# The last fold in pieces with a gate ahead of its transposes, finer weight turns and one more yield in a Fourier-mixing and expert kernel

## Chip, cores, metric

The kernel runs on one core of a Trainium2 chip. The metric is the time of the device in microseconds (us) for one execution; less is better. Each kernel was executed several times on one chip together with the kernel before, so that the two can be compared on the same chip. Each run has a state, fast or slow; on this one core a run counts as slow when it is over 1.5% above the fastest of its kernel. Medians and ranges below are of all runs of a kernel, ratios of its fast runs alone.

The engines are called as the profile calls them: PE is the tensor engine's matmuls (PEld its weight loads), DVE the vector engine, ACT the scalar engine, POOL GpSimd, SP the engine that issues most of the strip transfers. PSUM buffers are the buffers into which PE writes its results; to evict one is to copy it out, so that it can be used again. The granted clock is the share of full speed at which PE was allowed to run; where it is half, the text calls PE or the stretch cold, and warm where it is full.

## The reference

Two layers follow each other. The first takes the real part of a two-dimensional Fourier transform of each of 8 batches (2496 x 256). The second gives each of the 19968 rows to one of 8 experts, greedily by score and with equal capacity, and puts the row through that expert's two matrices. The code is shortened:

```python
def _attn_ref(x):                       # x: 8 x 2496 x 256
    X = np.fft.fft(x, axis=1)
    X = np.fft.fft(X, axis=2)
    return X.real.astype(np.float32)

def _moe_ref(x, w_gate, w1, w2):        # x: 19968 x 256, w1: 8 x 256 x 1024
    cap = N // E
    order = np.argsort(-(x @ w_gate).flatten())
    for idx in order:                   # greedy, each row once, each expert at most cap rows
        tok, e = (int(idx) // E, int(idx) % E)
        if assigned[tok] >= 0 or counts[e] >= cap:
            continue
        assigned[tok] = e
        counts[e] += 1
    # ... (cut: stop when all are assigned)
    for e in range(E):
        mask = assigned == e
        out[mask] = np.maximum(x[mask] @ w1[e], 0.0) @ w2[e]
```

## The kernel before

The program runs in stages, and these names are used throughout:

1. *Batches.* For each batch, DVE folds the rows with their mirror images (tiles `xa`, `xb`), PE transposes the result (`tp`) and multiplies it with the gate (`yps`), ACT copies.
2. *Logits.* PE transforms the gated columns along the sequence (`lps_...`).
3. *Selection and transform.* DVE chooses the rows of each expert by search, ranks and masks. Meanwhile PE computes the transform of the rows in 40 half-steps that are called units (`fftps`), and DVE, ACT and POOL combine them into strips which go to DRAM. PE also turns the first weights of four experts (`wps`: each turn is eight matmuls in four pairs, and each pair is evicted by ACT).
4. *Experts.* PE gathers, sorts (`sps`) and multiplies (`hps`, `ops`). In its midst an inverse list is built from one-hot matrices (`inv_ps`).

The last batch, as the kernel before emits it:

```python
for b in range(B):
    a_t, b_t = ab.pop(b)
    nc.vector.tensor_tensor(a_t[:, :, :, 1:D], a_t[:, :, :, 1:D], b_t[:, :, ::-1, D - 1:0:-1], op=AL.add)
    nc.vector.tensor_tensor(a_t[:, :, :, 0], a_t[:, :, :, 0], b_t[:, :, ::-1, 0], op=AL.add)
    # ... (cut)
    if b == B - 1:
        # ... (cut: the memory of xb is given to the weights)
        load_w1(0)
        load_w1(1)
        load_w2(wts[0])
        load_w2(wts[0])
    # ... (cut: copies and combinations of ACT and DVE)
    zts[b] = [turn_x(b, pv, 0), turn_x(b, pv, 1)]      # transposes of chunks 0 and 1
    if b > 0:
        gate_x(b - 1, zts.pop(b - 1))                  # gate of the batch ahead
    zts[b].append(turn_x(b, pv, 2))                    # transposes of chunk 2
    # ... (cut)
```

While the selection runs, the order of PE's work is decided when the program is built, by two counters of estimated time, `clock["PE"]` and `clock["D"]` (DVE). A `yield` with a number is so much DVE work; `yield SYNC` marks the place of a PE instruction of the selection, which waits for DVE.

```python
def unit():
    cost = next(units, None)
    if cost is not None:
        clock["PE"] += 1.15
        clock["D"] += cost
        clock["n"] += 1
        if clock["n"] in (18, 22, 28, 34):
            turn_w((18, 22, 28, 34).index(clock["n"]), "A")   # a whole expert in one block
            clock["PE"] += 2.0
    return cost is not None

for c in first_chain():
    if c is not SYNC:
        clock["D"] += c
        while clock["PE"] < clock["D"] - 1.0 and unit():
            pass
        continue
    # ... (cut: the same filling, then both counters are set to the later one)
```

In the expert stage, each yield of the generator `inverse` lets PE go on with one more part of other work before the inverse's own matmuls:

```python
yield 0.9
yield SYNC
for c in range(8):
    nc.tensor.matmul(inv_ps[:, 0:w], lhsT=o_lo[:, :, c], rhs=o_hi[:, c, :], ...)
```

## Time and profile before

| | kernel before |
|---|---|
| plain runs, median of 3 | 548.45 us (547.43 to 548.97) |
| profiled run, span | 591.5 us |
| PE busy | 482.5 us, 82% of the span |
| first expert matmul | at 173.79 us |
| longest wait of PE in the expert stage up to 360 us | 5.40 us, at the inverse |

The head of the profile's page: the busy time of each engine with its share of the span, and two rows of the span in 40 slices of 14.8 us. A digit is the busy share of a slice in tenths; PEclk is the granted clock of PE in tenths, so 9 is full.

```profile
PE 482.5 (82%) x4014; PEld 358.1 (61%) x4023; DVE 383.4 (65%) x1063; ACT 341.7 (58%) x786; POOL 310.8 (53%) x362
...
PE   0567778887899999998998798887787679687993
...
PEclk9998779999999999999999799999998989989997
```

The selection and transform lie in slices 7 to 11, where PE has sevens to nines, mostly eights; the expert stage behind them is nearly full up to the middle. From about 360 us on (slice 25) there are sevens and eights again, which the plain runs can hardly have had: the profiled execution was 43 us longer than they were. Behind 345 us PE has 17 waits of over 1 us in this profile, 30.8 us in sum. In the hole that is shown here PE, DVE and ACT are all idle for 1.7 us, and the profile does not name what ended it. The table of stretches shows it (window, its length, then the busy us of PE, PEld, DVE, ACT and POOL with counts, granted clock, share and GB/s of the DMA engines):

```profile
448.00:450.00 2.00, 0.37 (x3) 0.10 (x1) 0.00 (x0) 0.00 (x0) 0.52 (x1) 1.00 0.26 94
```

Why some executions have these holes, and on two chips all that were profiled, is not settled here. They are in kernels with and without the change. So what the change does is read from the first 340 us, in which the profiles are alike, and from times on one chip.

### The profile page before, as it was taken

The numbers are of one execution on the slowest core, as the hardware profiler recorded it, in microseconds if no ns is written. First come the engines' busy times: TensorE is split into PE (matmuls) and PEld (weight loads), VectorE is DVE, ScalarE is ACT, GpSimd is POOL, SyncE is SP. The second block draws the span as 40 slices with busy tenths as digits, with TensorE's granted clock in tenths as the row PEclk, the third lists the DMA queues.
The fourth block names the chain that finished last, engine by engine and source line by source line (L and its number), as shares of the span: only waits on it lengthen the run. The fifth ranks groups of instructions, "written<-read, shape, count | busy, mean of one in ns | idle before, by whom it ended". The sixth has DMA issues, their size and how long they took to land. (4 is left out here: it accounts for less than half of the span.)

```text
span 591.5 us, 11322 instructions
## 1 busy us (share of the span) xinstructions
PE 482.5 (82%) x4014; PEld 358.1 (61%) x4023; DVE 383.4 (65%) x1063; ACT 341.7 (58%) x786; POOL 310.8 (53%) x362
## 2 busy tenths in 40 slices
PE   0567778887899999998998798887787679687993
PEld 0444447775686667766765676655565457465772
DVE  7799864978889889798888762543332324343551
ACT  7789861454688778786777476443432334343551
POOL 7878540622226545343444245665666575656553
PEclk9998779999999999999999799999998989989997
DMA  8999835387698962222222223212222221112111
GB/s 270 314 282 305 252 62 83 109 292 207 203 280 162 240 148 90 91 94 89 89 90 95 69 89 98 71 54 76 66 65 70 67 75 55 61 53 66 65 55 48
DMA packets 35169, 74.63 MB, mean 126 GB/s; under 512 B 6115, under 2 KB 14349, under 8 KB 35104
## 3 DMA queue, kind: packets, MB, share of 16 engines
q0 software_dynamic: 23296, 42.10, 27.4%
q1 hardware_dynamic: 11808, 31.73, 15.9%
q8 instruction: 33, 0.54, 0.4%
q14 instruction: 32, 0.26, 0.1%
HBM read 51.26 MB, written 32.24 MB: 141 GB/s over the span
## 5 line engine op out<-in xcount | busy, mean ns | idle before, releaser
L990 ACT ACTIVATE hb<-hps 128x384 bf16<-128x384 f32 (+1 forms) x331 | 145.8, 492 | 77.1 <-PE hps L1229 61.0
L1252 PE MATMUL ops<-w2t,hb 128*128 128x256 bf16 (+1 forms) x1344 | 178.1, 277 | 0.1
L1252 PEld LDWEIGHTS <-hb 128*128 128x128 bf16 (+1 forms) x1344 | 134.3, 100 | 35.2 <-issue 1.9
L1256 POOL DMA_INDIRECT out_dram<-zball,rid x94 | 96.2, 1024 | 109.6 <-ACT zball L990 96.2
L1229 PE MATMUL hps<-xs,zball 128*128 128x384 bf16 x640 | 131.5, 330 | 19.3 <-issue 10.5
L1229 PEld LDWEIGHTS <-zball 128*128 128x128 bf16 x896 | 86.6, 99 | 87.0 <-issue 48.2
L994 DVE TENSOR_SCALAR hb<-hps 128x384 bf16<-128x384 f32 (+1 forms) x117 | 62.4, 546 | 69.4 <-PE hps L1229 45.2
L1229 PE MATMUL hps<-xt,zball 128*128 128x384 bf16 (+1 forms) x256 | 51.4, 329 | 16.8 <-issue 10.9
L990 ACT ACTIVATE zball<-ops 128x256 f32<-128x256 f32 x96 | 36.9, 385 | 46.8 <-PE ops L1252 26.0
L129 POOL DMA_INDIRECT xb<-in_x_dram,mir_i x40 | 53.0, 1326 | 14.0 <-issue 10.8
L285 PE MATMUL tp<-identf,xa 128*128 128x128 f32 x160 | 28.6, 345 | 21.2 <-issue 11.6
L990 ACT ACTIVATE xs<-sps 128x384 bf16<-128x384 f32 x73 | 32.4, 493 | 20.0 <-PE sps L1093 11.5
L285 PEld LDWEIGHTS tp<-identf,xa 128*128 128x128 f32 x160 | 24.2, 180 | 28.8 <-issue 13.9
L1093 PE MATMUL sps<-pt,xl 128*128 128x192 bf16 x320 | 34.4, 248 | 2.8 <-DVE pt L1071 1.8
L1021 POOL COPY stage<-stage 128x258 bf16<-128x258 bf16 x40 | 17.7, 446 | 35.8 <-DVE stage L1016 32.6
L1071 DVE TENSOR_SCALAR pt<-rampw,spot 128x193 bf16<-128x193 bf16 x160 | 32.2, 293 | 1.0 <-PE sps L1093 0.7
L1093 PEld LDWEIGHTS <-xl 128*128 128x128 bf16 x320 | 27.5, 99 | 8.1 <-issue 6.0
L1256 POOL DMA_INDIRECT out_dram<-zball,rows_l x23 | 22.3, 971 | 17.0 <-DVE zball L996 9.9
L996 DVE COPY zball<-ops 128x256 f32<-128x256 f32 (+1 forms) x21 | 8.9, 423 | 30.0 <-PE ops L1252 9.6
L1205 POOL DMA_INDIRECT xg<-t_dram,ids_l x24 | 23.1, 964 | 7.9 <-issue 7.9
L1019 ACT ACTIVATE stage<-stage 128x254 bf16<-128x254 bf16 x40 | 15.7, 414 | 15.8 <-DVE stage L1016 13.9
L287 ACT COPY zt<-tp 128x1024 f32<-128x1024 f32 (+1 forms) x24 | 20.2, 868 | 6.1 <-PE tp L285 6.1
(357 smaller groups left out, 783.5 us busy)
## 6 DMA issues: line engine op xcount, KB each, us to landing
t_dram<-stage SPq DMA_DIRECT2D x20, 512.0 KB
xl<-t_dram SPq DMA_DIRECT2D x20, 512.0 KB
xa<-in_x_dram SPq DMA_DIRECT2D x8, 1024.0 KB
w1raw<-in_moe_w_dram POOLq DMA_DIRECT2D x8, 512.0 KB
w2t<-in_moe_w_dram POOLq DMA_DIRECT2D x8, 512.0 KB
xa<-in_x_dram SPq DMA_DIRECT2D x8, 224.0 KB
out_dram<-zball,rid POOLq DMA_INDIRECT x94
xb<-in_x_dram,mir_i POOLq DMA_INDIRECT x40
```

The source lines that it names most:

```text
L129: nc.gpsimd.indirect_dma_start(out=bv[0:n, i, :], out_offset=None, in_=x_pairs, in_offset=bass.IndirectOffsetOnAxis(ap=mir_i[0:n, b * NK + ...
L285: nc.tensor.transpose(tp[:, blk, u, :], pv[:, 4 * c + u, blk * P:(blk + 1) * P], identf)
L287: nc.scalar.copy(zt[:, :, 0:nn, :], tp[:, :, 0:nn, :])
L990: nc.scalar.activation(dst, src, ACT.Relu if relu else ACT.Copy)
L994: nc.vector.tensor_scalar(dst, in0=src, scalar1=0.0, scalar2=None, op0=AL.max)
L1021: nc.gpsimd.tensor_copy(st[:, :, 1 + q, 0:P + 1], st[:, :, 3 * q, 0:P + 1])
L1071: nc.vector.tensor_scalar(marks[n][:, f, 0:EW + 1], in0=rampw[:, 0:EW + 1], scalar1=spot[:, c:c + 1], scalar2=None, op0=AL.is_equal)
L1093: nc.tensor.matmul(sps[:, j2 * EW:(j2 + 1) * EW], lhsT=xl[:, 2 * g + cc, j2 * P:(j2 + 1) * P], rhs=pt[:, 2 * g + cc, 0:EW], start=(cc == 0 ...
L1205: nc.gpsimd.indirect_dma_start(out=xg[0:nr, q, :], out_offset=None, in_=t_dram, in_offset=bass.IndirectOffsetOnAxis(ap=d["ids"](q, nr), ax ...
L1229: nc.tensor.matmul(hps[:, 0:n], lhsT=w1t[d["e"]][:, j2, fc * P:(fc + 1) * P], rhs=d["x"](j2), start=(j2 == 0), stop=(j2 == 1))
L1252: nc.tensor.matmul(ops[0:nr, 0:D], lhsT=d["hid"][:, fc, b0:b0 + nr], rhs=w2t[d["e"]][:, fc, :], start=(fc == 0), stop=(fc == F // P - 1))
L1256: put = nc.gpsimd.indirect_dma_start(out=out, out_offset=bass.IndirectOffsetOnAxis(ap=d["rows"](b0 // P)[0:nr], axis=0), in_=ot[0:nr, :], ...
```

## The change

Its intent was to shorten three places where PE waits: 2.29 us under the last fold, 1.51 and 2.10 us in the weight turns and 5.40 us at the inverse, in the profile before. The last fold goes in three pieces, so that the first transposes need not await all of it, and the gate of the batch ahead goes in front of those transposes, with its matmuls in another order (both halves of a chunk after each other). The weight turns of the first four experts go in sixteen pieces of two matmuls, one behind each of sixteen chosen units, so that no block of eight fills the PSUM buffers or stands in front of the search. And the inverse gets one more yield before its first matmuls.

```diff
     def gate_x(b, zts):
-        for blk in range(2):
-            for c, zt in enumerate(zts):
+        for c, zt in enumerate(zts):
+            for blk in range(2):
...
     for b in range(B):
         a_t, b_t = ab.pop(b)
-        nc.vector.tensor_tensor(a_t[:, :, :, 1:D], a_t[:, :, :, 1:D], b_t[:, :, ::-1, D - 1:0:-1], op=AL.add)
-        nc.vector.tensor_tensor(a_t[:, :, :, 0], a_t[:, :, :, 0], b_t[:, :, ::-1, 0], op=AL.add)
+        for i0, i1 in ((0, 2), (2, 4), (4, NK)) if b == B - 1 else ((0, NK),):
+            nc.vector.tensor_tensor(a_t[:, i0:i1, :, 1:D], a_t[:, i0:i1, :, 1:D], b_t[:, i0:i1, ::-1, D - 1:0:-1],
+                                    op=AL.add)
+            nc.vector.tensor_tensor(a_t[:, i0:i1, :, 0], a_t[:, i0:i1, :, 0], b_t[:, i0:i1, ::-1, 0], op=AL.add)
...
+        if b == B - 1:
+            gate_x(b - 1, zts.pop(b - 1))
         zts[b] = [turn_x(b, pv, 0), turn_x(b, pv, 1)]
-        if b > 0:
+        if 0 < b < B - 1:
             gate_x(b - 1, zts.pop(b - 1))
...
             yield SYNC
+            if c0 == 0:
+                yield SYNC
             for c in range(8):
                 nc.tensor.matmul(inv_ps[:, 0:w], ...)
...
     (turn_pieces is the body of turn_w, with a yield behind each pair of matmuls)
+    TURNS = (*range(15, 23), *range(26, 30), *range(33, 37))
+    pieces = (None for e in range(4) for _ in turn_pieces(e, "A"))
...
-            if clock["n"] in (18, 22, 28, 34):
-                turn_w((18, 22, 28, 34).index(clock["n"]), "A")
-                clock["PE"] += 2.0
+            if clock["n"] in TURNS:
+                next(pieces)
+                clock["PE"] += 0.45
```

More of the change, by code (lines that the diff above doesn't have):

```diff
@@ L1047, in turn_w, with turn_pieces @@
     def turn_w(e, eng=None):
+        for _ in turn_pieces(e, eng):
+            pass
+    def turn_pieces(e, eng=None):
         for j in range(2):
@@ L1055, in turn_w @@
                 take(w1t[e][:, j, fs], wps, eng=eng)
-        if e + 2 < E:
-            load_w1(e + 2)
+                if j == 1 and fh == 1 and e + 2 < E:
+                    load_w1(e + 2)
+                yield
     flat = [zball[:, b].rearrange("p i d -> p (i d)") for b in range(B)]
```

## The prediction

> **What bounds the kernel now.** I read four views: the stretches table (busy time of each engine in chosen windows), to see which engine is full where; the timeline around the last fold; the timeline around the weight turns; and the waits of the tensor engine (PE). The profiled execution took 591.5 us and the plain runs 548.45 us, so profiled stretches are up to 8% long in sum; I use differences only. Three rows of the stretches table (window, its length, then busy us of PE, PE weight loads, DVE, ACT, POOL, with counts):
>
> ```profile
> 62.00:82.00 20.00, 12.80 (x73) 8.05 (x74) 17.56 (x24) 15.95 (x36) 6.39 (x5) 0.77 0.44 141
> 125.00:152.00 27.00, 20.13 (x148) 14.16 (x149) 22.41 (x60) 13.07 (x28) 6.41 (x14) 1.00 0.61 180
> 174.00:200.00 26.00, 25.88 (x184) 17.44 (x185) 24.23 (x86) 21.94 (x54) 14.14 (x16) 1.00 1.02 205
> ```
>
> Up to about 150 us the PE has holes (12.80 of 20, 20.13 of 27); from there on it is full (25.88 of 26), and the chain that ended last is PE matmuls back to 355 us. So a microsecond in which the PE does not stand idle before the expert tiles, or between them, is a microsecond off the end; a microsecond won on DVE alone is not.
>
> The last batch (timeline):
>
> ```profile
> 78.86 2.81 DVE L343 TENSOR_TENSOR xa<-xa,xb 128x2550 f32<-128x2550 f32 x1
> 81.86 3.65 PE L285 MATMUL tp<-identf,xa 128*128 128x128 f32 x16 [2.29 <-issue]
> 85.44 2.33 PE L295 MATMUL yps<-zt,g_sb 128*32 128x512 f32 x12
> 88.83 1.91 PE L295 MATMUL yps<-zt,g_sb 128*32 128x512 f32 x12
> 92.67 0.19 PE L452 MATMUL lps_cE<-yhl,hi_cE 128*128 128x64 bf16 x1 [0.74 <-DVE yhl L309]
> ```
>
> The fold starts as soon as DVE is free (the DVE timeline shows no idle before it), so no load bounds it. PE idles 2.29 us under it, then transposes, does the gate of batch 6, then batch 7's gate, and the logits begin at 92.67. All is one chain.
>
> The weight turns and the late wait (timelines, and two more rows):
>
> ```profile
> 126.41 1.46 PE L1053 MATMUL wps<-w1raw,mt_b 128*128 128x512 bf16 x5
> 129.38 0.59 PE L1053 MATMUL wps<-w1raw,mt_b 128*128 128x512 bf16 x2 [1.51 <-ACT zball L990]
> 130.04 0.22 DVE L660 SCALAR_TENSOR_TENSOR s_low<-misc,s_part,s_lo 128x1 f32<-128x1 f32 x1 [1.65 <-PE misc L658]
> 136.72 0.22 DVE L660 SCALAR_TENSOR_TENSOR s_low<-misc,s_part,s_low 128x1 f32<-128x1 f32 x1 [1.95 <-PE misc L658]
> 151.69 0.59 PE L1053 MATMUL wps<-w1raw,mt_b 128*128 128x512 bf16 x2 [2.10 <-ACT zball L990]
> 328.46 0.64 PE L761 MATMUL inv_ps<-o_eq,oh 128*128 128x48 bf16 x8 [5.40 <-DVE o_eq L757]
> ```
>
> A turn's eight matmuls come in one block. The block outruns its three PSUM buffers and waits for ACT (1.51 and 2.10 us), and the search's one-column matmul (misc) behind it keeps DVE waiting (1.65, 1.95 us). At 328.46 the PE has waited 5.40 us, its longest wait of the expert stage, for the first one-hot of the inverse list.
>
> [...] 16 transposes take 1.94 us at 72.55 but 3.65 us at 81.86, and the granted clock of 62 to 82 us is 0.77. [...] In two narrow windows of batch 7's gate:
>
> ```profile
> 89.70 0.62 PE L295 MATMUL yps<-zt,g_sb 128*32 128x256 f32 x3
> 89.71 1.03 PE L295 MATMUL yps<-zt,g_sb 128*32 128x512 f32 x4
> ```
>
> A 256-wide matmul of chunk 2, the last in program order, starts at 89.70, while two 512-wide ones written before it still start after 90.1 (the group ends at 90.74). [...] I expect the new order to keep the 1.91 us. [...]
>
> **The change, part by part.**
>
> *Fold in pieces.* [...] Neighbours overlap by some 85 ns (78.86 to 81.76 is 2.90 for 2.985), five times instead of once: about 3.2 us, ending near 82.06 instead of 81.76. DVE loses 0.3 us, but pieces for chunks 0 and 1 are ready near 80.2 and 81.5. That readers wait for a slice only is visible elsewhere: the ACT copy of the stage tile starts at 109.52, before DVE's second write of that tile ends at 110.08.
>
> *Gate 6 first.* Its last input (the ACT copy at 79.03 to 79.61) is there, so it fills the PE's idle: 79.65 to 81.56 if warm, to about 83.1 if cold. Then, warm: transposes 81.5 to 83.45 (16 x 121 ns); ACT does the border copy after the fold (82.05), the two gate copies (to 82.95), the chunk copies of 1.0 us to 83.9 and 84.85; the last four transposes follow the first copy, then the place step to 85.05; batch 7's gate runs 84.95 to 86.85. From the gate's end to the logits took 90.74 to 92.67 = 1.93: logits near 88.8, a gain of 3.9. If the clock drops near 79.5, as it did before: gate 6 ends at 83.1, and the logits come near 90.2, a gain of 2.5. I take 3.3.
>
> *Weight turns.* I replayed the program's own pacing counters, which decide where units go. Before, 30 units (1.11 us of PE each) and three turns are issued in the first selection; after, 29 units and twelve pieces (the same three turns). Two pieces (2 x 0.43 us) now stand before the first search, which starts 0.87 later; the two search answers come near 129.2 and 132.7 instead of 130.04 and 136.72, and DVE reaches the strip marks about 4.7 us earlier. But PE is what counts. Idle removed: 1.51 + 2.10 in the turns, 0.53 at the rank matmuls, 0.28 at a stage buffer. Idle added: DVE's threshold and mask steps are no longer covered (1.30 to about 1.6, 0.99 to 2.0), about 0.8 behind one late piece eviction, 0.4 at a rank buffer, and 1.1 when a unit needs a PSUM buffer whose combine is queued behind the strip marks. That is 4.4 removed against 3.6 added, 0.8. Followed step by step to equal work (30 units, three turns), PE arrives near 153.3 instead of 154.4: 1.1. The fourth turn saves perhaps 0.4, which ACT, then nearly full, may take back. I take 1.1 in all.
>
> *One more yield in the inverse.* PE gets one more part of work ahead of the first inverse matmuls: eight sorting matmuls (0.66), six up (0.97), eight down (0.87) = 2.5 us off the 5.40. The remaining 3 us still cools the clock, as the 5.4 did, so I add nothing for it. The late gathers start one part later and are far from needed.
>
> Sum: 3.3 + 1.1 + 2.5 = 6.9 us. The rest of the program stays in order and PE-bound. 548.45 - 6.9 = 541.5.
>
> **Rivals.** (a) The gate's column groups serialize in the new order[...]. Then each gate has four steps of 0.43 per large chunk, about 3.5 us instead of 1.9; with gates 6 and 7 both on the chain the first part gains 0.7 at most, the total 4.3: 544. The narrow windows speak against it. (b) The units trade one wait for another: DVE's gain becomes PE idle at its masks and PSUM buffers, and twelve short evictions fill ACT. Then the turns give nothing or cost 1: 542.5 to 543.5. For it speaks that PE's idle sum hardly changes in my replay. (c) The saved DVE time does come through, because PE waits on DVE later (the waits of the expert stage up to 360 us, the inverse aside, sum to only 6.6 us): a turn gain near 4 makes 538.5. (d) The clock: PE stays warm through the last batch and the shorter inverse wait saves the half-rate stretch (sorting 1.45 against 0.82, up 2.08 against 1.14, 1.6 us): 539.5.
>
> **Range and chances.** The three gains are 2 to 4, -0.5 to 3 and 1.5 to 4; not all at one end. That makes 538.5 to 545. Faster by over 2% means under 537.5, a gain of 11, for which all three must be at their best: 0.08. A loss over 2% needs a mechanism that I see nowhere: 0.01.
>
> **What would show it.** In the profile after: no PE idle of 2 us before the last transposes, gate 6 ahead of them, and the first logits matmul 2.5 to 3.9 us earlier; one gate still near 1.9 us when warm (near 3.5: rival a). No wait of PE in the turns on ACT over 1 us, search answers without a DVE wait on misc near 1.7, and new PE waits on the masks near 2 us. The inverse wait near 3 us instead of 5.4. The prediction is wrong if the logits come less than 1.5 us earlier, if the PE reaches the first expert tile no earlier relative to the logits than before (rival b) or over 3 us earlier (rival c), or if the inverse wait stays.

## The result, and the profile after

The changed kernel is correct. It takes 543.83 us (median of 4 runs, 543.31 to 545.83), against 548.55 us of the kernel before beside it. Ratios here are the mean time of one kernel's fast runs over that of the other's in the same rounds, so they are not quite the ratio of the medians. The ratio is 0.9924, with a 95% interval of 0.9895 to 0.9953: 4.7 us faster, which is "the same" by the measure that counts only changes over 2%. It lies inside the predicted range, 2.3 us slower than the predicted 541.5.

The head of the page after, span 542.1 us, slices of 13.6 us:

```profile
PE 469.0 (87%) x4023; PEld 355.7 (66%) x4023; DVE 387.2 (71%) x1067; ACT 345.2 (64%) x786; POOL 312.4 (58%) x362
...
PE   0667777796899999999899989999999999999970
...
PEclk9997889999999999999999998999999999999995
```

The late slices are at nine or above: this execution has no late holes. Comparing the two spans would credit the change with 49 us; the comparison has to be made mark by mark.

The last batch in the timeline after (start us, duration us, engine, source line, operation, output<-inputs, sizes, count, and in brackets the idle time before it and what ended it):

```profile
77.78 1.21 DVE L344 TENSOR_TENSOR xa<-xa,xb 128x1020 f32<-128x1020 f32 x1
...
79.10 1.92 PE L295 MATMUL yps<-zt,g_sb 128*32 128x512 f32 x12
...
80.95 1.97 PE L285 MATMUL tp<-identf,xa 128*128 128x128 f32 x16
...
84.16 1.92 PE L295 MATMUL yps<-zt,g_sb 128*32 128x512 f32 x12
...
88.03 0.19 PE L456 MATMUL lps_cE<-yhl,hi_cE 128*128 128x64 bf16 x1 [0.74 <-DVE yhl L309]
```

The gate of batch 6 now stands before the transposes and takes 1.92 us, as does that of batch 7 in the new order. The transposes run at full clock (1.97 us instead of 3.65). From the fold's first piece to the logits it is 88.03 - 77.78 = 10.25 us, where it was 92.67 - 78.86 = 13.81.

Behind that, three waits of PE decided the rest. They lie inside the logits, at the threshold of the selection, and at the inverse (lines of the timeline after):

```profile
94.56 0.19 PE L456 MATMUL lps_cO<-yhl,hi_cO 128*128 128x64 bf16 x1 [1.51 <-issue]
...
132.41 0.29 PE L840 MATMUL lev_ps<-identf,s_lev 128*128 128x128 f32 x1 [2.99 <-DVE stage L1023]
...
325.94 0.64 PE L767 MATMUL inv_ps<-o_eq,oh 128*128 128x48 bf16 x8 [2.74 <-DVE o_eq L761]
```

The first is new: PE stands still for 1.51 us in the middle of matmuls that wait for no other engine. The second is of the selection's own matmul behind the search, which now has to await a combination that DVE makes for a unit; before, this wait was 1.30 us. The third is what is left of the 5.40 us.

To add such gains up, take five marks that every kernel has: the start of the last fold, the first logits matmul, the first unit, the first expert matmul (`hps`), the 337th of those (just before the inverse), and the 241st sorting matmul (`sps`, just behind it). The table gives the us between marks, from one profiled execution each.

| kernel | fold to logits | logits to first unit | first unit to experts | experts to before the inverse | across the inverse | sum |
|---|---|---|---|---|---|---|
| before | 13.81 | 10.13 | 71.00 | 147.26 | 18.96 | 261.16 |
| after | 10.26 | 11.79 | 70.95 | 147.76 | 15.73 | 256.49 |
| after, repeated (r1) | 11.27 | 11.91 | 71.18 | 147.79 | 15.94 | 258.07 |
| e1 yield alone | 13.31 | 10.15 | 71.02 | 147.22 | 15.94 | 257.64 |
| e2 fold and gate alone | 10.27 | 11.91 | 71.03 | 147.23 | 18.94 | 259.36 |
| e3 turns alone | 13.86 | 10.13 | 70.97 | 148.30 | 19.93 | 263.19 |
| e4 as e2, weights later (slow run) | 12.50 | 10.13 | 78.25 | 147.30 | 18.91 | 267.08 |
| e6 after, second yield | 10.26 | 11.70 | 71.10 | 147.79 | 12.63 | 253.48 |
| e7 gate first alone | 10.18 | 11.72 | 71.03 | 147.46 | 18.99 | 259.38 |
| e8 after, cheaper pieces | 11.27 | 11.91 | 69.42 | 147.19 | 16.99 | 256.79 |
| e9 after, w2 later | 10.26 | 10.13 | 71.35 | 147.81 | 15.93 | 255.47 |
| e10 after, turns undone | 9.81 | 11.68 | 71.03 | 147.21 | 14.48 | 254.21 |
| b1 e6 + e8 + e9 | 11.26 | 10.13 | 69.36 | 147.50 | 12.64 | 250.89 |
| b2 b1, third yield | 11.22 | 10.13 | 69.34 | 147.29 | 11.02 | 249.00 |

Each row is one execution, and the same work differs between executions where the clock fell differently: across the inverse, before and e3 have the same wait of 5.40 us, and take 18.96 and 19.93 us.

From before to after the columns give 3.55 - 1.66 + 0.05 - 0.50 + 3.23 = 4.67 us. The plain runs give 548.55 - 543.83 = 4.72. Behind the last mark the profile of before has 251 us and that of after 208; with 208 in place of 251 the kernel before would come to 340.02 + 208 = 548 us, which is what its plain runs take.

### The profile page after: what moved, and what is told of

Read it like the earlier page. It is cut to its first block, busy times and chain, and to the rows that moved or that the text cites. A ratio compares the mean times of both kernels' runs of the same rounds, so it can differ in the third digit from the quotient of the medians.

```text
span 542.1 us, 11340 instructions
## 1 busy us (share of the span) xinstructions
PE 469.0 (87%) x4023; PEld 355.7 (66%) x4023; DVE 387.2 (71%) x1067; ACT 345.2 (64%) x786; POOL 312.4 (58%) x362
## 5 line engine op out<-in xcount | busy, mean ns | idle before, releaser
L1265 PE MATMUL ops<-w2t,hb 128*128 128x256 bf16 (+1 forms) x1344 | 174.3, 273 | 0.0
L1265 PEld LDWEIGHTS <-hb 128*128 128x128 bf16 (+1 forms) x1344 | 132.8, 99 | 32.1 <-issue 0.3
L1242 PE MATMUL hps<-xs,zball 128*128 128x384 bf16 x640 | 127.3, 327 | 0.3 <-ACT hb L996 0.2
L1242 PEld LDWEIGHTS <-zball 128*128 128x128 bf16 x896 | 85.2, 98 | 45.1 <-issue 4.3
L1000 DVE TENSOR_SCALAR hb<-hps 128x384 bf16<-128x384 f32 (+1 forms) x117 | 63.5, 548 | 42.4 <-PE hps L1242 34.0
L129 POOL DMA_INDIRECT xb<-in_x_dram,mir_i x40 | 55.0, 1376 | 11.9 <-issue 10.2
L996 ACT ACTIVATE zball<-ops 128x256 f32<-128x256 f32 (+1 forms) x97 | 37.3, 384 | 37.0 <-PE ops L1265 32.8
L1242 PE MATMUL hps<-xt,zball 128*128 128x384 bf16 (+1 forms) x256 | 47.7, 319 | 0.0
L1045 ACT COPY ev<-fftps 128x512 f32<-128x512 f32 x20 | 11.6, 582 | 19.4 <-PE fftps L1039 10.4
```

The costliest lines, as they stand in the source:

```text
L129: nc.gpsimd.indirect_dma_start(out=bv[0:n, i, :], out_offset=None, in_=x_pairs, in_offset=bass.IndirectOffsetOnAxis(ap=mir_i[0:n, b * NK + ...
L996: nc.scalar.activation(dst, src, ACT.Relu if relu else ACT.Copy)
L1000: nc.vector.tensor_scalar(dst, in0=src, scalar1=0.0, scalar2=None, op0=AL.max)
L1242: nc.tensor.matmul(hps[:, 0:n], lhsT=w1t[d["e"]][:, j2, fc * P:(fc + 1) * P], rhs=d["x"](j2), start=(j2 == 0), stop=(j2 == 1))
L1265: nc.tensor.matmul(ops[0:nr, 0:D], lhsT=d["hid"][:, fc, b0:b0 + nr], rhs=w2t[d["e"]][:, fc, :], start=(fc == 0), stop=(fc == F // P - 1))
```

## The experiments

Twelve runs were made, in three calls on three chips. All gave correct results. On the second chip the kernel before took 548.15 us; on the first and the third it took 600.55 and 598.0 us, with single runs 8 to 12 us apart. Every profile taken on those two has the late holes (12 to 18 waits of PE of over 1 us behind 345 us, 27 to 40 us in sum); after, r1, e6, e8 and e9 have none. There the times of small parts drown, and the columns of the table speak. They speak for the first 340 us only: on the first chip e2 and e4 came out slower than the kernel before, with intervals of the ratio wholly above 1, and what made them slower is not shown. Of the 75 runs of the kernel before there, 24 count as slow.

**e1: the yield alone.** The kernel before, with

```diff
             yield SYNC
+            if c0 == 0:
+                yield SYNC
```

> The kernel before with one thing added: the second yield ahead of the first inverse matmuls. My theory: PE puts 2.5 us of work into its 5.40 us wait, so the time falls by 2.5 to 3.5 us (the profiles of before and after differ by 3.2 across this place). Rival: the late tiles' gathers start a part later and give it back, 0 to 1 us.

Measured: 599.33 us against 600.55 (ratio 1.0017, 0.9991 to 1.0042). The profile's timeline:

```profile
328.07 0.64 PE L763 MATMUL inv_ps<-o_eq,oh 128*128 128x48 bf16 x8 [2.74 <-DVE o_eq L757]
```

The wait is 2.74 us, as in the changed kernel, and the way across the inverse 15.94 instead of 18.96. So the yield alone is worth 3.0 us there, and needs no other part of the change. The fall of the time that was expected is not seen; on this chip the time cannot show it.

**e2: fold and gate alone.** The kernel before, with the first three hunks of the change.

> The kernel before with the fold in pieces, the gate of batch 6 first and the new gate order, nothing else. Fold to first logits matmul 10.2 us instead of 13.8. In the profile after, 1.51 us of that are lost again in a hole inside the logits matmuls, where a 16 KB instruction packet was fetched just as the four early weight loads landed. Theory A (the earlier logits run into the weight loads, which hold the fetch up): the hole is here again, gain about 2.0 us. Theory B (the hole is chance): no hole, gain about 3.6 us.

Measured: 601.79 us against 600.55 (1.0041, 1.0013 to 1.007). Fold to logits 10.27, as in the changed kernel; but logits to first unit 11.91 instead of 10.13. The hole is there again:

```profile
96.77 0.19 PE L456 MATMUL lps_cO<-yhl,hi_cO 128*128 128x64 bf16 x1 [1.62 <-issue]
```

So it comes with the fold and gate, and takes half of their gain back. The time did not show the rest, it rose by 0.4%.

**e3: turns alone.** The kernel before, with `turn_pieces`, `TURNS` and the new `unit`.

> The kernel before with the weight turns in pieces, nothing else. My theory from the two profiles: PE's idle time only moves (8.8 us before and 8.9 after between the first unit and the first expert tile), a new 3 us wait at the level transposition takes the place of the two waits on ACT: 0, within 1 us either way. Rival (c) of the prediction: DVE's lead comes through later, 3 to 4 us faster. Step as predicted: 1.1 us faster.

Measured: 603.17 us against 600.55 (1.0029, 0.9988 to 1.0071). First unit to experts takes 70.97 instead of 71.00: nothing gained. The next column, experts to before the inverse, takes 148.30 instead of 147.26: 1.0 lost.

**e4: e2 with the first four weight loads later.**

```diff
         if b == B - 1:
-            load_w1(0)
-            load_w1(1)
-            load_w2(wts[0])
-            load_w2(wts[0])
...
+    load_w1(0)
+    load_w1(1)
+    load_w2(wts[0])
+    load_w2(wts[0])
+
     def payloads(i, dst):
```

> As e2, with the four early weight loads moved in program order behind the logits, so that they are issued when the logits end. Theory A: the hole is gone, and the logits take 10.2 us to the first unit instead of 11.8; about 1.5 us faster than e2. Theory B: the same as e2 within 0.5 us. If the loads are needed sooner than I think, the first weight turn (near 126 us) waits for them and it is slower.

Measured: 607.15 us against 600.55 (1.0057, 1.0019 to 1.0095); its profiled run was one of the slow state, so only its waits are read. Logits to first unit is back at 10.13, without a hole: moving the loads removes it. But they are now issued at 108 to 110 us, among the strips. A line of its timeline:

```profile
122.25 0.69 DVE L1021 TENSOR_TENSOR stage<-ev,fftps 128x512 bf16<-128x512 f32 x1 [4.62 <-DMA t_dram<-stage]
```

DVE waits 4.62 us for a strip's store to leave its buffer, and PE behind it; the stage takes 78.25 us. Moving the loads took the hole away, but the gain over e2 that was expected did not come: this was the wrong place for them.

**r1: the changed kernel again**, unaltered, on the chip of e6, e8 and e9.

> The changed kernel once more, unaltered, as the baseline of the three others on their chip. Theory: its ratio to the kernel before is that of the first measurement, 0.992, give or take 0.003, and from the first fold piece to the first logits matmul it takes 10.3 us, from there to the first transform unit 11.8. Rival: 0.992 was a difference between single runs, and the ratio comes out at 0.997 or more.

Measured: 543.72 us (543.39 to 545.91, 6 runs) against 548.15; ratio 0.9919, 0.9901 to 0.9936. The result stands. Its profiled run was the slowest of its six, and shows one reason why single runs differ:

```profile
78.59 3.61 PE L295 MATMUL yps<-zt,g_sb 128*32 128x512 f32 x12
```

Here gate 6 ran at half clock (3.61 us instead of 1.92), and fold to logits took 11.27 instead of the expected 10.3. It is the same program, 1.0 us apart in this stretch by its clock.

**e6: a second extra yield.**

```diff
             if c0 == 0:
                 yield SYNC
+                yield SYNC
```

> The changed kernel with one more extra yield before the first matmul of the inverse. Theory: the 2.74 us that TensorE still waits there goes to 0 to 0.5, the 3.4 us of cold clock after it goes too, and from the inverse's first matmul's place to the expert tiles behind it 2.5 to 4 us are gained. Rival: VectorE's own chain sets the inverse, the wait moves to another matmul behind it, and under 1 us is gained.

Measured: 541.05 us against 548.15; ratio 0.9866, 0.9847 to 0.9885; 2.7 us less than r1.

```profile
325.61 0.62 PE L768 MATMUL inv_ps<-o_eq,oh 128*128 128x48 bf16 x8 [1.22 <-DVE o_eq L761]
```

The wait shrank by 1.5, not to nothing, and yet the way across the inverse shrank from 15.94 to 12.63, by 3.3, because the clock no longer fell: the granted clock was 1.00 from 322 to 334 us, where r1 had worked 3.41 us at half (half of that, 1.7, and the 1.5 make 3.2). The theory missed the size of the wait and met the gain, since it had counted the clock too.

**e8: the pieces accounted at less.**

```diff
-                clock["PE"] += 0.45
+                clock["PE"] += 0.2
```

> The changed kernel with a piece of a weight turn accounted at 0.2 us in place of 0.45, so that the transform units fall about where they fell before. Theory: the transform stage lost what it gained because the lev_ps matmul now comes right behind a unit whose combination VectorE still owes; the wait of 2.99 us at lev_ps shrinks to under 1.5, and first unit to first expert matmul goes from 70.95 to 69.5 to 70.0 us. Rival: the sum of TensorE's waits in that stage is set by VectorE's own work, one wait is traded for another, and it stays within 0.5 us of 70.95.

Measured: 540.65 us against 548.15; ratio 0.9856, 0.9836 to 0.9876; 3.1 us less than r1. First unit to experts takes 69.42 instead of 71.18, and the first third of the experts 147.19 instead of 147.79. Two waits of PE in the stage, in all, times and longest, in the table of waits from 101.2 to 171 us:

```profile
PE lev_ps L840 <- DVE s_lev L835: 1.9, 1, 1.9
PE wps L1063 <- ACT zball L996: 1.8, 2, 1.0
```

`lev_ps` now waits for its own input and not for a combination of a unit; 1.88 us is more than the 1.5 expected, but the stage gained what was expected. The number that tells the program how long a piece takes was wrong for its purpose, and 0.25 us in it is worth 1.5 us (against the first profile of the changed kernel) to 1.8 us (against r1) in this stage. Both profiled runs were the slowest of their kernels: they differ by 1.2 us, and their sums in the table by 1.3, since e8 was cold for longer across the inverse (6.8 us at half clock, against 3.41 in r1). The rest of the 3.1 us between the medians was not profiled.

**e9: the w2 loads behind the logits.** The w1 loads stay; a copy of one element makes the queue of the w2 loads wait (they are issued at 92.59 us, in the changed kernel at 82.73).

```diff
             load_w1(1)
-            load_w2(wts[0])
-            load_w2(wts[0])
...
         for n in ("cE", "sE"):
             nc.scalar.copy(even[n], lps[n])
+        nc.gpsimd.tensor_copy(pool6[0][:1, 1000:1001], even["sE"][:1, 0, 0:1])
+        load_w2(wts[0])
+        load_w2(wts[0])
```

> The changed kernel with the loads of the first two w2 weights held back until the logits' first copies are done (a one-element GpSimd copy makes them wait); the w1 loads stay where they are. Theory: the 1.51 us hole of TensorE inside the logits is an instruction fetch held up behind the weight loads; with half of them gone the fetch comes 1.5 to 2.5 us after the first logits matmul instead of 4.1, the hole goes to about 1.1, and logits to first unit takes 10.1 to 10.6 us instead of 11.8; nothing behind it moves by more than 0.5. Rival: the fetch is late for another reason, the 11.8 stays. Second rival: the w2 loads now hold up the next fetch or a strip store, and the gain is lost again within 15 us.

Measured: 542.89 us against 548.15; ratio 0.9904, 0.9882 to 0.9925. Logits to first unit takes 10.13. Stretches of the changed kernel, where the weights are on their way until 94 us (the last two numbers are DMA share and GB/s; the share can exceed 1, for a packet's whole time is counted where it starts):

```profile
90.00:92.00 2.00, 2.00 (x74) 2.00 (x71) 1.65 (x15) 0.43 (x1) 0.00 (x0) 1.00 1.45 197
92.00:94.00 2.00, 1.05 (x36) 0.95 (x33) 0.00 (x0) 0.43 (x1) 0.00 (x0) 1.00 1.42 194
```

and of this one:

```profile
88.00:90.00 2.00, 2.00 (x74) 2.00 (x71) 1.79 (x10) 0.24 (x1) 0.00 (x0) 1.00 0.03 8
92.00:94.00 2.00, 2.00 (x74) 2.00 (x71) 0.00 (x0) 0.39 (x1) 1.54 (x3) 1.00 0.03 8
```

In the trace, the 16 KB packet of the instruction queue starts 4.07 us after the first logits matmul in the changed kernel (92.10) and 1.51 us after it here (88.87). In the kernel before it was 1.98. PE is busy all through, where a hole of 1.1 had been expected to stay. In all seven profiles that have the hole, PE goes on 1.46 to 1.49 us after this packet has landed; that ties the hole to the packet. The first theory holds for its place: 1.66 to 1.78 us are gone. The time fell by only 0.8 us; next to it, first unit to experts is 0.2 to 0.4 longer, and the runs of r1 and e9 spread over 2.5 and 3.2 us. So the second rival is not wholly excluded for a part of the gain.

**e7: gate first alone.** The kernel before, with one hunk.

```diff
+        if b == B - 1:
+            gate_x(b - 1, zts.pop(b - 1))
         zts[b] = [turn_x(b, pv, 0), turn_x(b, pv, 1)]
-        if b > 0:
+        if 0 < b < B - 1:
```

> The kernel before with one part of part 1 alone: the gate of batch 6 is emitted ahead of the transposes of batch 7; the fold stays whole and the gate keeps its order of matmuls. Theory: in the changed kernel the 16 transposes begin where gate 6 ends, 3.2 us after the fold begins, which is also where the whole fold ends (2.98 us), so the three pieces and the new matmul order are worth nothing, and first fold to first logits matmul takes 10.0 to 10.5 us with the clock full during gate 6, 11.0 to 11.5 with it at half, as in the changed kernel; ratio to before 0.993 to 0.996. Rival: the pieces carry part of the gain, and it takes 12 us or more of the kernel before's 13.8.

Measured: 597.74 us against 598.0 (0.9989, 0.9962 to 1.0017), on a chip with late holes; 0.993 to 0.996 had been expected. Fold to logits takes 10.18 us, no more than with the pieces. Its timeline:

```profile
78.38 2.81 DVE L343 TENSOR_TENSOR xa<-xa,xb 128x2550 f32<-128x2550 f32 x1
...
79.67 1.91 PE L295 MATMUL yps<-zt,g_sb 128*32 128x512 f32 x12
...
81.51 1.97 PE L285 MATMUL tp<-identf,xa 128*128 128x128 f32 x16
```

Here a fold in one piece is followed by transposes 3.13 us after its start; in the changed kernel they came 3.17 us after it. The gate put in front carries the gain alone; the pieces and the new order of its matmuls add nothing here.

**e10: the turns undone.** The changed kernel with `turn_w` and `unit` of before.

> The changed kernel with its weight turns as in the kernel before (whole experts at four places); fold, gate and the extra yield stay. Theory: the turns in pieces are worth nothing or cost some tenths of a microsecond, so first unit to first expert matmul stays at 70.7 to 71.2 us, and the time is within 1.5 us of the changed kernel's 543.7, ratio to before 0.990 to 0.993. Rival: the pieces gave the 1.1 us that the prediction counted, and the stage is longer by that and the time 544.8 or more.

Measured: 594.11 us against 598.0; ratio 0.9926, 0.9896 to 0.9956, about the ratio of the whole change on other chips. First unit to experts 71.03, experts to before the inverse 147.21: the turns in pieces gave nothing and cost 0.5 afterwards. Two further columns differ by luck of the clock. Gate 6 found its inputs 0.64 us after the fold's start (in the changed kernel 1.32), so the transposes began 2.48 us after it: only here can the pieces of the fold have helped, by some 0.4 (9.81 against 10.18 in e7). And the same wait at the inverse, 2.75 us, did not cool the clock:

```profile
325.00:328.00 3.00, 2.09 (x23) 1.75 (x23) 2.93 (x6) 0.87 (x2) 0.00 (x0) 1.00 0.13 44
328.00:331.00 3.00, 3.00 (x34) 2.40 (x33) 2.97 (x12) 2.02 (x5) 1.28 (x1) 1.00 0.14 46
```

In e8 the same two stretches, after a wait of 2.74 us, were granted half:

```profile
325.00:328.00 3.00, 2.86 (x18) 1.88 (x18) 2.93 (x7) 0.98 (x2) 0.00 (x0) 0.50 0.00 0
328.00:331.00 3.00, 3.00 (x19) 1.82 (x18) 2.16 (x10) 1.34 (x3) 0.97 (x1) 0.50 0.00 1
```

Across the inverse it took 14.48 us in e10, 15.73 in the changed kernel, 16.99 in e8: one wait of one length, 2.5 us apart.

**b1: all three mendings together** (e6, e8 and e9).

> The changed kernel with the second extra yield, the pieces accounted at 0.2 us, and the w2 loads held back until the logits are done. Theory: the three gains are of three stages and add up: 3.3 at the inverse, 1.8 in the transform stage, 1.6 in the logits, 6.7 in all less some clock phase, 537 to 538.5 us, ratio to before 0.979 to 0.983. Rival: they overlap or shift the clock's steps against each other and it stays at 539.5 to 540.5, no better than the pieces alone.

Measured: 586.78 us against 598.0; ratio 0.9801, 0.9745 to 0.9858; the verdict at 2% is unclear. The columns add up: against r1, with the gate cold in both, 1.78 + 1.82 + 0.29 + 3.30 = 7.2 us. The interval lies wholly below that of the changed kernel (0.9901 to 0.9936 in r1, on another chip), and on its own chip b1 is 7.3 us below e10. It beats the kernel before. That it beats the changed kernel is shown by the columns, and by e6 and e8 for two of its three parts; the two were not run on one chip, and its time without late holes was not measured.

**b2: a third yield on top**, one more line as in e6.

> The one before it with a third extra yield. Theory: the 1.22 us that TensorE still waits at the inverse after two goes to under 0.3 and 0.5 to 1.2 us more are gained, 536.5 to 538. Rival: the transform work that a yield moves is now longer than the wait, VectorE gets the inverse's chain later, and it is equal or slower by up to 1 us.

Measured: 592.9 us against 598.0; ratio 0.9878, 0.9818 to 0.9938. The wait at the inverse is 0.21 us, and the way across it 11.02 instead of 12.64, 1.6 gained where the theory had 0.5 to 1.2:

```profile
327.28 0.61 PE L770 MATMUL inv_ps<-o_eq,oh 128*128 128x48 bf16 x8 [0.21 <-DVE o_eq L762]
```

But the time is 6 us above that of b1. The loss lies behind 424 us, among the late holes: at the 561st expert matmul b2 is still ahead, 424.61 against 424.81 us, and at the last one 4.6 us behind, 577.34 against 572.75. Whether the third yield helps where there are no holes is open.

## Why the prediction was right, and where not

The predicted 541.5 us was off by 2.3, and the range held the result. The sum of 6.9 us is to be set against the 4.7 measured, by its own steps. By one of the signs that it named itself it was wrong: PE reaches the first expert matmul 82.75 us after the first logits matmul, where it was 81.12, so 1.6 later and not earlier. The range held because it was wide enough for what one step lost and another left out, not because these were foreseen together.

**Fold and gate, predicted 3.3 (2.5 with a cold clock, 3.9 with a warm one).** The gain was 3.55 us with the clock full, in the first profile, and 13.81 - 11.27 = 2.54 with it at half, in r1. Mechanism and size were right, with both cases met. The old order was never seen warm: in before, e1 and e3 the clock was half for 3.4 to 6.8 us of this stretch, and the smallest gain between two profiles in the fast state is 13.31 - 11.27 = 2.0. The step about the pieces was right in size (3.16 us of fold; the 3.2 predicted were the author's estimate, and a straight line through the two ops of the kernel before, 2815 ns for 2550 elements and 170 for 10, gives as an estimate 1222 ns for a piece of 1020, where 1.21 us was measured) but had no part in the gain: e7 shows that the gate in front is all of it, since gate 6 ends just when the fold does (only in e10, where the gate could start sooner, some 0.4 may be theirs). A piece of work that is ready sooner is worth something only if its reader is free sooner.

**What the step left out: the instruction packet.** "The rest of the program stays in order and PE-bound" was the failing sentence. The logits came 3.55 us sooner, but the weight loads did not: they wait for the fold to free the memory of `xb` (the first was issued 3.20 us after the fold's start before, 3.46 after). So the logits now ran beside the loads, and a packet of 16 KB of the instruction queue started 4.07 us after the first logits matmul, where it had been 1.98. It is taken for a fetch of PE's instructions, because PE stands still until 1.46 to 1.49 us after it has landed in the seven profiles that have the hole; the trace does not name its engine. The stretch from the logits to the first unit grew by 1.66 us. The hole is there in every profile with the early logits and early loads (after, r1, e2, e6, e7, e8, e10: 11.68 to 11.91 us), and in none with later loads (e4, e9, b1, b2: 10.13) or later logits (before, e1, e3: 10.13 to 10.15). That it is the loads that hold the packet up is shown by e4 and e9, which differ from e2 and r1 in the place of the loads alone.

**Weight turns, predicted 1.1 (rival b: nothing, or a loss).** Rival b was right. First unit to experts went from 71.00 to 70.95; e3 (the turns alone, 70.97) and e10 (all but the turns, 71.03) agree that nothing was gained. What was removed went as predicted: the waits of 1.51 and 2.10 us on ACT became one of 0.80, and the search answers came at 126.21 and 129.75 us, 0.9 and 4.0 us sooner relative to the first unit, with no wait for `misc` before them. But PE's idle sum in the stage stayed (8.76 before, 8.87 after). The term that was mis-sized is the wait at the threshold, taken as "about 1.6": it was 2.99 us, since `lev_ps` shares a PSUM buffer with a unit and found one there whose combination DVE had only just begun when the input of `lev_ps` was ready (130.98 and 131.06 us). Behind it, in the first expert tiles, PE had two waits of 0.23 and 0.27 us that it had not had before; they make the 0.5 that the next column lost. e8 shows that the place of the units, not the pieces as such, was at fault: with the pieces accounted at 0.2 us the stage takes 69.42 us, 1.6 less than before the change, more than the 1.1.

**The yield, predicted 2.5.** The wait fell by 5.40 - 2.74 = 2.66, as computed from three durations. The way across gained 3.0 to 3.2. The cold stretch was halved (3.41 us instead of 6.83), but that explains little of the rest, for the first half of the long one lay in the wait itself. Two stretches of the kernel before, and one after:

```profile
325.26:328.45 3.19, 0.00 (x0) 0.14 (x1) 2.81 (x10) 0.00 (x0) 0.00 (x0) 0.50 0.12 41
328.46:332.07 3.61, 3.60 (x22) 2.49 (x22) 3.30 (x6) 1.85 (x4) 0.00 (x0) 0.50 0.19 45
...
325.94:329.04 3.10, 3.10 (x19) 2.06 (x19) 3.03 (x6) 0.98 (x2) 0.00 (x0) 0.50 0.00 0
```

PE worked at half clock for 3.61 us before and 3.10 after (3.41 in e1 and r1), which at half speed is 0.1 to 0.25 us. So the step that added nothing for the clock was nearly right; of the 0.5 to 0.7 above 2.5, 0.16 is the wait, and about 0.3 stays unexplained.

**The rivals.** (a) fell: gate 7 takes 1.92 us in the new order, 1.91 in the old; its 256-wide matmuls, last in program order, start at 84.54 us, before the last 512-wide ones at 85.47. (c) fell with the turns. (d) was true in part, now here, now there (the last batch was warm in after; in r1 its first gate was cold, 3.61 us instead of 1.92). In before and after every stretch of one granted clock but the last is a whole number of steps of 3.41 us; across the inverse it was half for 6.83 us from 325.25 us before, and for 3.41 us from 325.63 us after. The waits of 2.74 or 2.75 us in e10, after and e8 went with no cold step, one and two (across the inverse 14.48, 15.73 and 16.99 us). So such a wait had no fixed price here; it cost 0 to 2.5 us beyond itself. A step need not be idle throughout for the clock to be half behind it: before, PE was busy for 1.24 of the 3.41 us from 321.83 us, and after for 0.98 of those from 322.22 us. Laid on the grid of the steps, from 60 to 345 us of the 14 profiles, each of the 29 full-clock steps in which PE was idle for 2.0 us or more was followed by a cold one, none of those with under 1.55 us, and some of those between (12 of 36). In e10 the edge of a step, at 324.75 us, cut the wait into 1.59 and 1.16 us; in e8 2.00 us of it fell into one step.

In sum, in us: 6.9 predicted, less 1.66 for the hole, less 1.55 for the turns (1.1 gained became 0.45 lost), more 0.25 for the fold and gate and 0.73 for the yield makes 4.67, beside 4.72 measured. Two readings were off without effect: the warm transposes start at 72.58 (72.55 is their weight load), and the profile was long only behind 360 us.

## What to carry to other kernels

When a change makes one engine's chain arrive sooner, ask what does not move with it; here the weight loads kept their time, and a packet of the instruction queue came 4.07 us after the first logits matmul instead of 1.98. Work moved into the gaps of a pacing program was worth nothing here until the program's cost number was set anew; look also at the buffers that its pieces share (`lev_ps` waited 2.99 us for one). A wait behind which the clock fell was worth more than its length here: the second yield took 1.5 us off a wait and gained 3.3. Of six waits of 2.74 or 2.75 us at the inverse five were followed by cold work; the shorter ones, of 1.22, 1.24 and 0.21 us (e6, b1 and b2), were not.
